# Last block's second layer in rounds of its own, its last stores on two queues; first block: a later load of the next x, weight joins in other slots

## The chip, the cores and the metric

The kernel runs on one core of one Trainium2 chip. The metric is the device time of one execution in microseconds (us), lower is better. The trace's span is about 1.8 us shorter than the device time of the same execution; where I follow one instruction I use the span's clock, which starts at zero with the first instruction. A transfer's landing is the moment when its counter says that it has finished; landings near the end of the kernel are taken to 0.01 us from the counters in the packed traces, since the views give them to 0.1. The close is the time from the last landing to the end of the span.

## The reference

A causal convolution over 7 steps, one softmaxed filter for each of 8 heads, then a two-layer network with hardswish:

```python
w = softmax(weight)                                    # (8, 7)
x1[b, s, d] = sum_k w[head(d), k] * x_padded[b, s + k, d]   # x: (8, 4096, 192)
h = x1.reshape(32768, 192) @ w_in                      # (192, 2048), float64 on input
g = h * clip(h + 3, 0, 6) / 6
out = g @ w_out                                        # (2048, 192), float64 on input
```

## The kernel before

The 32768 tokens go in 32 blocks of 1024. For each block VectorE convolves, TensorE makes h in PSUM banks (8 of 512 columns), ScalarE makes `r6 = relu(h/6 + 1/2)`, VectorE gates it (`g = min(r6, 1) * h`) and so frees the bank, and TensorE multiplies g by `w_out`. From block 1 on, both layers use Strassen's seven products instead of eight; block 0 is direct, since it also converts the weights. Words of 64 bits are loaded into `stage`, split on VectorE, scaled on ScalarE ("clamp"), joined on VectorE and multiplied on GpSimd, for 16 units: 0 to 7 are `w_in`, 8 to 15 `w_out`.

Block 0, the part that the change touches:

```python
swap(thirds[1]); split(3); split(4); join(2); clamp(3)   # join(n) also issues load(n + 4)
x_tiles[1] = load_x(1)
...
slots = [0, 1, 2, 3, 4, 6, 8, 10, 12, 14]    # a unit is joined in these slots
n = 3
for slot, (c, group) in enumerate(parts):    # slots 0 to 3 hold all 8 banks from the start
    ...                                      # TensorE: 6 matmuls into two banks
    def between():
        if more:
            join(n); clamp(n + 1)
    h_out(c, group, bs, ...)                 # two relus, between(), two gates that free the banks
    if more:
        split(n + 2)
        ...                                  # slots 0 to 3: between() comes here
        n += 1
```

The second layer of a later block, from which the last one differed only by having no next convolution:

```python
b, bank = three(1, 2, 0)       # one bank: product 1 on 96 partitions, a third of product 2 on 32
...
b, bank = three(4, 2, 1)
...                            # product 2's last third, in quarters of the contraction
b7, bank7 = three(7, 5, 0)
b, bank = three(6, 5, 1)
...                            # u2 = p1 + p6, u3 = u2 + p7, p4 = u3 - p4, store
b, bank = three(3, 5, 2)
piece(p5, 2, bank, NQ)         # ScalarE copies product 5's last third out of the bank
add(u2[:], u2[:], bank[m])     # VectorE, the other 96 partitions of the same bank
give(b)
add(u2[:], u2[:], p5[:])
store(u2, 0, 1)                # a transpose on VectorE, then three stores of 64 KB on SyncE's queue
add(u3[:], u3[:], p5[:])
store(u3, 1, 1)
```

Of the kernel before, what the change touches and what calls it, by code (L numbers as in the profile page):

```python
# [8 lines left out]
ALU = mybir.AluOpType  # L9
# [7 lines left out]
def kernel(  # L17
# [255 lines left out]
    def swap(part):  # L273

        to = slice(OTHER + part.start, OTHER + part.stop)
        nc.sync.dma_start(out=y[D2:P, to], in_=y[0:D2, part])
        nc.sync.dma_start(out=y[0:D2, to], in_=y[D2:P, part])
# [19 lines left out]
    def take():  # L297
        return free_banks.pop(0)
# [131 lines left out]
    def side_by_side(*streams):  # L430
        for mms in zip(*streams):
            for m in mms:
                m()

    every = range(NP)

    def store_rows(i, k, q, xt, j):

        t0 = i * TB + k * N
        nc.sync.dma_start(  # L440
            out=out[t0 : t0 + N, q * QS : (q + 1) * QS].rearrange("(t r) d -> r t d", r=QS),
            in_=xt[j * QS : (j + 1) * QS].rearrange("r (t d) -> r t d", d=QS),
        )
# [28 lines left out]
    def g_sums(engine, which, slots, width):  # L472
# [5 lines left out]
        for n in which:  # L478
            o, a, b, op = forms[n]
            for p in slots[::width]:  # L480
                r = slice(p, p + width)
                engine.tensor_tensor(out=o[:, r], in0=a[:, r], in1=b[:, r], op=op)  # L482

    def out_strassen(i, conv):

        prod = {
            1: (A11, B11), 2: (A12, B21), 3: (S4, B22), 4: (A22, T4),
            5: (S1, T1), 6: (S2, T2), 7: (S3, T3),
        }

        def product(bank, j, n, q, ks=every):
            return mm(bank, j, *prod[n], q, ks, True, True)

        def three(n, n4, q4):
            b = take()
            bank = psum[:, b]
            side_by_side(
                *[product(bank, q, n, q) for q in range(NQ)], product(bank, NQ, n4, q4)
            )
            return b, bank  # L500

        def piece(dst, q, src, j):
            nc.scalar.copy(  # L503
                out=dst[q * QS : (q + 1) * QS], in_=src[j * QS : (j + 1) * QS]
            )

        def add(out, x, y, op=ALU.add):
            nc.vector.tensor_tensor(out=out, in0=x, in1=y, op=op)  # L508

        def store(c, k, half_):  # L510

            xt = ot.tile([P, N], F32, name="xt")
            nc.vector.transpose(out=xt[0:DH], in_=c[:])  # L513
            for q in range(NQ):
                store_rows(i, k, half_ * NQ + q, xt, q)

        m = slice(0, DH)
        p1, p2, p4, p5, u2, u3 = (cs.tile([DH, N], F32, name=f"c{k}") for k in range(6))
        for u in conv:
            u()  # L520
        b, bank = three(1, 2, 0)
        nc.scalar.copy(out=p1[:], in_=bank[m])  # L522
        piece(p2, 0, bank, NQ)
        give(b)
        g_sums(nc.vector, (2,), every, 4)
        b, bank = three(4, 2, 1)
        nc.scalar.copy(out=p4[:], in_=bank[m])  # L527
        piece(p2, 1, bank, NQ)
        give(b)
        if conv:  # L530
            swap(slice(0, K3))
        n = NP // 4
        b = take()
        bank = psum[:, b]
        side_by_side(*[product(bank, j, 2, 2, range(j * n, (j + 1) * n)) for j in range(4)])
        last = slice(2 * QS, 3 * QS)
        piece(p2, 2, bank, 0)
        for j in range(1, 4):
            add(p2[last], p2[last], bank[j * QS : (j + 1) * QS])
        give(b)  # L540
        g_sums(nc.vector, (4,), every, 4)
        add(p2[:], p1[:], p2[:])
        store(p2, 0, 0)
        b7, bank7 = three(7, 5, 0)
        piece(p5, 0, bank7, NQ)
        if conv:
            y_sums()
        b, bank = three(6, 5, 1)
        piece(p5, 1, bank, NQ)
        add(u2[:], p1[:], bank[m])  # L550
        give(b)
        add(u3[:], u2[:], bank7[m])
        give(b7)
        add(p4[:], u3[:], p4[:], ALU.subtract)
        store(p4, 1, 0)
        b, bank = three(3, 5, 2)
        piece(p5, 2, bank, NQ)
        add(u2[:], u2[:], bank[m])
        give(b)
        add(u2[:], u2[:], p5[:])  # L560
        store(u2, 0, 1)
        add(u3[:], u3[:], p5[:])
        store(u3, 1, 1)

    def split(n):
        if n < len(units):
# [15 lines left out]
    with tc.manual_schedule():  # L582
        nc.vector.tensor_reduce(out=sm[:], in_=e_sb[:], axis=AX.X, op=ALU.add)
        nc.vector.tensor_scalar_add(sm[:], sm[:], 1e-9)
        nc.vector.reciprocal(sm[:], sm[:])
        nc.vector.tensor_tensor(
            out=c_sb[:], in0=e_sb[:], in1=sm[:].to_broadcast([P, KC]), op=ALU.mult
        )

        thirds = [slice(s, s + 1) for s in range(K3)]  # L590
        pe_third = K3 - 1
        b = take()
        for _ in range(3):

            nc.tensor.matmul(
                out=psum[:, b], lhsT=zeros[:, 0:P], rhs=zeros[:], start=True, stop=True
            )
        for k in range(KC):
            nc.scalar.mul(diag[:, k], ident[:], c_sb[:, k : k + 1])
            nc.tensor.matmul(  # L600
                out=psum[:, b], lhsT=diag[:, k], rhs=x_tiles[0][:, pe_third, k : k + N],
                start=(k == 0), stop=(k == KC - 1),
            )
        conv0 = conv_units(0, thirds[:pe_third], 2)
        per = len(conv0) // pe_third
        for k, u in enumerate(conv0):
            if k == 5:
                split(0)
                clamp(0)
            elif k == per - 3:  # L610
                join(0, more=False)
            elif k == per:
                nc.scalar.copy(out=y[:, pe_third], in_=psum[:, b])
                give(b)
                swap(thirds[0])
                swap(thirds[pe_third])
                load(AHEAD)
                split(1)
                clamp(1)
            elif k == per + 6:  # L620
                split(2)
                join(1)
                clamp(2)
            u()
        swap(thirds[1])
        split(3)
        split(4)
        join(2)
        clamp(3)
        x_tiles[1] = load_x(1)  # L630


        parts = [(c, group) for p in range(0, NP, 2) for group in (OWN, OTHER)
                 for c in (p, p + 1)]
        early = [(c, group, (take(), take())) for c, group in parts[:4]]
        order = (0, pe_third, 1)
        for c in range(2):
            for slot, group, bs in early:
                if slot == c:
                    for s in order[:2]:  # L640
                        h_mm(c, group, bs, s, order)
        for c, group, bs in early:
            h_mm(c, group, bs, order[2], order)

        slots = [0, 1, 2, 3, 4, 6, 8, 10, 12, 14]
        n = 3
        for slot, (c, group) in enumerate(parts):
            first = slot < len(early)
            if first:
                bs = early[slot][2]  # L650
            else:
                bs = take(), take()
                for s in range(K3):
                    h_mm(c, group, bs, s)
            more = slot in slots

            def between():
                if more:
                    join(n)
                    clamp(n + 1)  # L660

            h_out(c, group, bs, (lambda: None) if first else between)
            if more:
                split(n + 2)
                if first:
                    between()
                n += 1
        while n < len(units):
            join(n)
            clamp(n + 1)  # L670
            split(n + 2)
            n += 1
        w_sums()
        start_pools.close()
        ss = ctx.enter_context(tc.tile_pool(name="ss", bufs=1))
        p5s = ctx.enter_context(tc.tile_pool(name="p5s", bufs=3))
        cs = ctx.enter_context(tc.tile_pool(name="cs", bufs=1))
        ot = ctx.enter_context(tc.tile_pool(name="ot", bufs=4))

        def conv_and_swap(i):  # L680
            return conv_units(i, [slice(0, K3)]) + [lambda: swap(slice(0, K3)), y_sums]

        out_direct(0, conv_and_swap(1))
        x_tiles[2] = load_x(2)

        S1 = ss.tile([P, NP, N], F32, name="s1")[:]
        for i in range(1, NB):
            h_phase()
            out_strassen(i, conv_units(i + 1, [slice(0, K3)]) if i + 1 < NB else [])
            if i + 2 < NB:  # L690
                x_tiles[i + 2] = load_x(i + 2)

# [32 lines left out]
```

## Time and profile before

| | |
|---|---|
| time, median of 3 | 2446.81 us |
| TensorE busy | 2431.6 of 2444.9 us |
| TensorE idle before its first matmul / in block 0 / after its last | 1.5 / 3.5 / 8.3 us |
| second layer of block 0 begins | 60.94 us |
| last matmul ends | 2436.65 us |

The table is read as a budget: TensorE does the same work before and after, so only its idle time can change, and it lies at the two ends. The prediction below shows the lines.

### The profile page before, as it was taken

What the parts mean: (1) busy time and instruction counts of PE and PEld (TensorE: products, weight loads), DVE (VectorE), ACT (ScalarE), POOL (GpSimd) and SP (SyncE); (2) the same over time, 40 slices, a digit from 0 to 9 for tenths busy, and PEclk for the clock granted to TensorE, in tenths of its full rate; (3) what the DMA queues carried; (4) which work ended last, traced back from release to release, by engine and by line L of the source; (5) the groups of instructions that cost most, each with busy time, mean ns of one, the idle gap of its engine ahead of it and who ended that gap; (6) DMA issues with size and microseconds to landing.
All of it is one profiled execution on the core that took longest, in us unless ns stands there. A gap on an engine that the chain in (4) does not pass through costs nothing.

```text
span 2444.9 us, 40253 instructions
## 1 busy us (share of the span) xinstructions
PE 2431.6 (99%) x16468; PEld 1282.4 (52%) x16468; DVE 2089.3 (85%) x2532; ACT 1082.1 (44%) x1826; POOL 670.3 (27%) x280
## 2 busy tenths in 40 slices
PE   9999999999999999999999999999999999999998
PEld 4335554455554455544555445555455554455543
DVE  8788888988888888888888898888888888888885
ACT  7234553345443355433454334543335543345432
POOL 2423321233221333122332123322133312233222
PEclk9999999999999999999999999999999999999999
DMA  5211121101122111111112211122201122111210
GB/s 143 40 26 28 27 40 40 39 18 27 36 40 40 21 33 27 40 40 23 30 27 40 40 34 23 24 40 40 40 19 35 27 40 40 21 33 27 40 27 14
DMA packets 227338, 84.67 MB, mean 35 GB/s; under 512 B 205456, under 2 KB 210576, under 8 KB 227152
## 3 DMA queue, kind: packets, MB, share of 16 engines
q1 hardware_dynamic: 226904, 81.69, 16.7%
q8 instruction: 129, 2.11, 0.4%
q14 instruction: 57, 0.47, 0.1%
q0 software_dynamic: 96, 0.26, 0.0%
q10 hardware_dynamic: 152, 0.13, 0.0%
HBM read 31.72 MB, written 25.17 MB: 23 GB/s over the span
## 4 chain that ended last, share of the span: by engine, by line
PE 98%; DVE 1%; DMA 0%; issue 0%; SPq 0%; ACTq 0%; POOL 0%; ACT 0%; DVEq 0%
PE psum L311 51%; PE psum L422 48%; DMA stage<-in_moe_w_in_dram 0%; DVE y L263 0%; DMA x<-in_x_dram 0%; DVE sig L199 0%; DVE c L508 0%; DVE scale L195 0%; DVE scale L174 0%; DVE g L321 0%; DVE top L178 0%; ACTq L92 0%; POOL w_in L203 0%; DVE y L259 0%; DVE xt L513 0%
## 5 line engine op out<-in xcount | busy, mean ns | idle before, releaser
L422 PE MATMUL psum<-g,w_out 128*32 128x512 f32 x9312 | 1165.2, 592 | 0.0
L311 PE MATMUL psum<-y,w_in 64*128 64x512 f32 x3664 | 980.9, 591 | 3.5 <-DVE g L321 1.3
L422 PEld LDWEIGHTS psum<-g,w_out 128*32 128x32 f32 x9312 | 337.8, 110 | 812.9 <-issue 764.8
L482 POOL TENSOR_TENSOR s<-g 128x1024 f32<-128x1024 f32 x124 | 293.4, 2366 | 1676.3 <-DVE g L321 1632.2
L317 ACT ACTIVATE r<-psum,half 128x512 f32<-128x512 f32 x1024 | 637.1, 687 | 245.9 <-PE psum L311 242.9
L311 PEld LDWEIGHTS psum<-y,w_in 64*128 64x128 f32 x3664 | 615.3, 187 | 194.7 <-issue 69.2
L321 DVE SCALAR_TENSOR_TENSOR g<-r,psum 128x512 f32<-128x512 f32 x1024 | 642.6, 680 | 4.6 <-ACT r L317 1.8
L422 PE MATMUL psum<-s,w_out 128*32 128x512 f32 x1488 | 643.6, 592 | 0.0
L311 PE MATMUL psum<-y,w_in_t 64*128 64x512 f32 x1984 | 639.2, 595 | 0.0
L391 DVE TENSOR_TENSOR psum<-psum,p 128x512 f32<-128x512 f32 x496 | 320.9, 692 | 209.1 <-PE psum L311 202.1
L263 DVE SCALAR_TENSOR_TENSOR y<-x,c_sb,y 128x1536 f32<-128x1536 f32 (+1 forms) x210 | 416.7, 1991 | 6.6
L311 PEld LDWEIGHTS psum<-y,w_in_t 64*128 64x128 f32 x1984 | 336.1, 187 | 138.1 <-issue 28.2
L503 ACT COPY c<-psum 32x512 f32<-32x512 f32 x186 | 107.6, 578 | 602.4 <-PE psum L422 601.7
L482 POOL TENSOR_TENSOR g<-g 128x1024 f32<-128x1024 f32 x124 | 336.4, 2713 | 9.7
L508 DVE TENSOR_TENSOR c<-c,psum 32x512 f32<-32x512 f32 (+1 forms) x186 | 127.4, 685 | 103.1 <-ACT c L503 98.0
L384 ACT COPY psum<-psum 128x512 f32<-128x512 f32 x248 | 138.6, 571 | 64.9 <-PE psum L311 52.6
L387 ACT COPY p<-psum 128x512 f32<-128x512 f32 x248 | 141.8, 586 | 54.9 <-PE psum L311 51.4
L422 PEld LDWEIGHTS psum<-s,w_out 128*32 128x32 f32 x1488 | 163.7, 110 | 0.0
L482 DVE TENSOR_TENSOR g<-s,g 128x2048 f32<-128x2048 f32 x62 | 141.1, 2316 | 2.2 <-PE psum L422 2.2
L482 DVE TENSOR_TENSOR g<-g 128x2048 f32<-128x2048 f32 x62 | 139.3, 2288 | 1.0
L522 ACT COPY c<-psum 96x512 f32<-96x512 f32 x31 | 18.0, 581 | 197.4 <-PE psum L422 197.4
L527 ACT COPY c<-psum 96x512 f32<-96x512 f32 x31 | 18.0, 581 | 175.7 <-PE psum L422 175.7
(45 smaller groups left out, 433.4 us busy)
## 6 DMA issues: line engine op xcount, KB each, us to landing
out_dram<-xt SPq DMA_DIRECT2D x384, 64.0 KB, 2.0
y<-y SPq DMA_DIRECT2D x62, 384.0 KB, 4.9
x<-in_x_dram SPq DMA_DIRECT2D x55, 388.5 KB, 5.5
stage<-in_moe_w_in_dram SPq DMA_DIRECT2D x16, 192.0 KB, 5.3
stage<-in_moe_w_out_dram SPq DMA_DIRECT2D x8, 384.0 KB, 6.3
x<-in_x_dram SPq DMA_DIRECT2D x7, 384.0 KB, 4.7
y<-y SPq DMA_DIRECT2D x6, 128.0 KB, 2.3
x<-in_x_dram SPq DMA_DIRECT2D x2, 128.0 KB, 4.4
```

The costliest lines, as they stand in the source:

```text
L263: nc.vector.scalar_tensor_tensor(out=to, in0=x[:, part, k + t : k + t + W], scalar=c, in1=to, op0=ALU.mult, op1=ALU.add,)
L311: nc.tensor.matmul(out=psum[:, b], lhsT=w[r], rhs=y[r, third_of_y], start=start, stop=stop, skip_group_check=onto,)
L317: nc.scalar.activation(r6, h, ACT.Relu, bias=half[:], scale=1.0 / 6.0)
L321: nc.vector.scalar_tensor_tensor(out=out, in0=r6, scalar=1.0, in1=h, op0=ALU.min, op1=ALU.mult)
L384: nc.scalar.copy(out=psum[:, bank["b"]], in_=psum[:, bank["a"]])
L387: nc.scalar.copy(out=self.p5[:], in_=psum[:, bank["e"]])
L391: nc.vector.tensor_tensor(out=psum[:, to], in0=psum[:, bank["b"]], in1=self.p5[:], op=ALU.add)
L422: lambda p=p: nc.tensor.matmul(out=bank[j * QS : (j + 1) * QS], lhsT=w_out[:, p, w, cols], rhs=x[:, p], start=(first and p == ps_[0]), sto ...
L482: engine.tensor_tensor(out=o[:, r], in0=a[:, r], in1=b[:, r], op=op)
L503: nc.scalar.copy(out=dst[q * QS : (q + 1) * QS], in_=src[j * QS : (j + 1) * QS])
L508: nc.vector.tensor_tensor(out=out, in0=x, in1=y, op=op)
L522: nc.scalar.copy(out=p1[:], in_=bank[m])
```

## The change

The intent is to shorten both ends. In block 0 the next block's x is loaded behind the weights, which are more urgent, and the fourth join is moved one slot back. In the last block, which has no next convolution to serve, the products go in another order, so that only one add and a transpose stand between the last matmul and most of the stores, and these go out on two queues. The core of the diff; the helper functions moved out of `out_strassen`, with little change (`store` now takes its rows and queues):

```diff
-    def store_rows(i, k, q, xt, j):
+    def store_rows(i, k, q, xt, j, dma=nc.sync):
...
+    def out_last(i):
+        both = nc.sync, nc.scalar
...                                   # rounds (1 with a third of 2) and (two thirds of 2, of 4)
+        b7, bank7 = three(7, 5, 0)
+        piece(p5, 0, bank7, NQ)
+        b, bank = three(6, 5, 1)
+        piece(p5, 1, bank, NQ)
...                                   # u2, u3, two thirds of p4, two stores
+        b, bank = by_quarters(5, 2)
+        pieces(p5, 2, bank)
+        give(b)
+        add(u2[:], u2[:], p5[:])
+        add(p5[:], u3[:], p5[:])
+        store(i, p5, 1, 1)
+        b, bank = three(3, 4, 2)
+        add(u2[:], u2[:], bank[m])
+        store(i, u2, 0, 1, queues=both)
+        add(u3[rows(2)], u3[rows(2)], bank[rows(NQ)], ALU.subtract)
+        store(i, u3, 1, 0, range(2, 3), queues=both[::-1])
+        give(b)
...
-        x_tiles[1] = load_x(1)
...
-        slots = [0, 1, 2, 3, 4, 6, 8, 10, 12, 14]
+        slots = [0, 1, 2, 3, 5, 6, 8, 10, 12, 14]
...
+            if slot == 6:
+                x_tiles[1] = load_x(1)
             h_out(c, group, bs, (lambda: None) if first else between)
```

More of the change, by code (lines that the diff above doesn't have):

```diff
@@ L435 @@
     every = range(NP)
-    def store_rows(i, k, q, xt, j):
+    def store_rows(i, k, q, xt, j, dma=nc.sync):
         t0 = i * TB + k * N
-        nc.sync.dma_start(
+        dma.dma_start(
             out=out[t0 : t0 + N, q * QS : (q + 1) * QS].rearrange("(t r) d -> r t d", r=QS),
@@ L482, in g_sums @@
                 engine.tensor_tensor(out=o[:, r], in0=a[:, r], in1=b[:, r], op=op)
-    def out_strassen(i, conv):
-        prod = {
-            1: (A11, B11), 2: (A12, B21), 3: (S4, B22), 4: (A22, T4),
-            5: (S1, T1), 6: (S2, T2), 7: (S3, T3),
-        }
-        def product(bank, j, n, q, ks=every):
-            return mm(bank, j, *prod[n], q, ks, True, True)
-        def three(n, n4, q4):
-            b = take()
-            bank = psum[:, b]
-            side_by_side(
-                *[product(bank, q, n, q) for q in range(NQ)], product(bank, NQ, n4, q4)
-            )
-            return b, bank
-        def piece(dst, q, src, j):
-            nc.scalar.copy(
-                out=dst[q * QS : (q + 1) * QS], in_=src[j * QS : (j + 1) * QS]
-            )
-        def add(out, x, y, op=ALU.add):
-            nc.vector.tensor_tensor(out=out, in0=x, in1=y, op=op)
-        def store(c, k, half_):
-            xt = ot.tile([P, N], F32, name="xt")
-            nc.vector.transpose(out=xt[0:DH], in_=c[:])
-            for q in range(NQ):
-                store_rows(i, k, half_ * NQ + q, xt, q)
-        m = slice(0, DH)
-        p1, p2, p4, p5, u2, u3 = (cs.tile([DH, N], F32, name=f"c{k}") for k in range(6))
@@ new lines, with product, four, three @@
+    prod = {
+        1: (A11, B11), 2: (A12, B21), 3: (S4, B22), 4: (A22, T4),
+        5: (None, T1), 6: (S2, T2), 7: (S3, T3),
+    }
+    def product(bank, j, n, q, ks=every):
+        x, w = prod[n]
+        return mm(bank, j, S1 if n == 5 else x, w, q, ks, True, True)
+    def four(*parts):
+        b = take()
+        bank = psum[:, b]
+        side_by_side(*[product(bank, j, n, q) for j, (n, q) in enumerate(parts)])
+        return b, bank
+    def three(n, n4, q4):
+        return four(*[(n, q) for q in range(NQ)], (n4, q4))
@@ new lines, in by_quarters, with rows, piece, pieces @@
+    def by_quarters(n, q):
+        b = take()
+        bank = psum[:, b]
+        w = NP // 4
+        side_by_side(
+            *[product(bank, j, n, q, range(j * w, (j + 1) * w)) for j in range(4)]
+        )
+        return b, bank
+    def rows(q):
+        return slice(q * QS, (q + 1) * QS)
+    def piece(dst, q, src, j):
+        nc.scalar.copy(out=dst[rows(q)], in_=src[rows(j)])
+    def pieces(dst, q, src):
+        piece(dst, q, src, 0)
+        for j in range(1, 4):
+            add(dst[rows(q)], dst[rows(q)], src[rows(j)])
@@ new lines, in add, with store, sums_tiles @@
+    def add(out, x, y, op=ALU.add):
+        nc.vector.tensor_tensor(out=out, in0=x, in1=y, op=op)
+    def store(i, c, k, half_, qs=range(NQ), queues=(nc.sync,)):
+        xt = ot.tile([P, N], F32, name="xt")
+        r = slice(qs[0] * QS, (qs[-1] + 1) * QS)
+        nc.vector.transpose(out=xt[r], in_=c[r])
+        for q in qs:
+            store_rows(i, k, half_ * NQ + q, xt, q, queues[q % len(queues)])
+    def sums_tiles():
+        return (cs.tile([DH, N], F32, name=f"c{k}") for k in range(6))
@@ new lines @@
+    m = slice(0, DH)
+    def out_last(i):
+        both = nc.sync, nc.scalar
+        p1, p2, p4, p5, u2, u3 = sums_tiles()
+        b, bank = three(1, 2, 0)
+        nc.scalar.copy(out=p1[:], in_=bank[m])
+        piece(p2, 0, bank, NQ)
+        give(b)
+        g_sums(nc.vector, (2,), every, 4)
+        b, bank = four((2, 1), (2, 2), (4, 0), (4, 1))
+        for dst, q, j in ((p2, 1, 0), (p2, 2, 1), (p4, 0, 2), (p4, 1, 3)):
+            piece(dst, q, bank, j)
+        give(b)
+        g_sums(nc.vector, (4,), every, 4)
+        add(p2[:], p1[:], p2[:])
+        store(i, p2, 0, 0)
+        b7, bank7 = three(7, 5, 0)
+        piece(p5, 0, bank7, NQ)
+        b, bank = three(6, 5, 1)
+        piece(p5, 1, bank, NQ)
+        add(u2[:], p1[:], bank[m])
+        give(b)
+        add(u3[:], u2[:], bank7[m])
+        give(b7)
+        two = slice(0, 2 * QS)
+        add(p4[two], u3[two], p4[two], ALU.subtract)
+        store(i, p4, 1, 0, range(2))
+        b, bank = by_quarters(5, 2)
+        pieces(p5, 2, bank)
+        give(b)
+        add(u2[:], u2[:], p5[:])
[6 more added lines that the diff above has]
+        store(i, u3, 1, 0, range(2, 3), queues=both[::-1])
+        give(b)
@@ L519, in out_strassen @@
+    def out_strassen(i, conv):
+        p1, p2, p4, p5, u2, u3 = sums_tiles()
         for u in conv:
@@ L529, in out_strassen @@
         give(b)
-        if conv:
-            swap(slice(0, K3))
-        n = NP // 4
-        b = take()
-        bank = psum[:, b]
-        side_by_side(*[product(bank, j, 2, 2, range(j * n, (j + 1) * n)) for j in range(4)])
-        last = slice(2 * QS, 3 * QS)
-        piece(p2, 2, bank, 0)
-        for j in range(1, 4):
-            add(p2[last], p2[last], bank[j * QS : (j + 1) * QS])
+        swap(slice(0, K3))
+        b, bank = by_quarters(2, 2)
+        pieces(p2, 2, bank)
         give(b)
@@ L542, in out_strassen @@
         add(p2[:], p1[:], p2[:])
-        store(p2, 0, 0)
+        store(i, p2, 0, 0)
         b7, bank7 = three(7, 5, 0)
         piece(p5, 0, bank7, NQ)
-        if conv:
-            y_sums()
+        y_sums()
         b, bank = three(6, 5, 1)
@@ L554, in out_strassen @@
         add(p4[:], u3[:], p4[:], ALU.subtract)
-        store(p4, 1, 0)
+        store(i, p4, 1, 0)
         b, bank = three(3, 5, 2)
@@ L560, in out_strassen @@
         add(u2[:], u2[:], p5[:])
-        store(u2, 0, 1)
+        store(i, u2, 0, 1)
         add(u3[:], u3[:], p5[:])
-        store(u3, 1, 1)
+        store(i, u3, 1, 1)
     def split(n):
@@ L688 @@
             h_phase()
-            out_strassen(i, conv_units(i + 1, [slice(0, K3)]) if i + 1 < NB else [])
+            if i + 1 < NB:
+                out_strassen(i, conv_units(i + 1, [slice(0, K3)]))
+            else:
+                out_last(i)
             if i + 2 < NB:
```

## The prediction

> **What bounds the kernel now.** I read the page's head first, then TensorE's order of time over the first 100 us, then VectorE, ScalarE and the SyncE queue in the same stretch, then the chain that ended last over the final 10 us.
>
> ```profile
> span 2444.9 us, 40253 instructions
> PE 2431.6 (99%) x16468; PEld 1282.4 (52%) x16468; DVE 2089.3 (85%) x2532; ACT 1082.1 (44%) x1826; POOL 670.3 (27%) x280
> ```
>
> TensorE is idle for 2444.9 - 2431.6 = 13.3 us in all. The table of stretches gives TensorE 2300.00 of 2300.00 us between 100 and 2400 us at a granted clock of 1.00, so whatever the 30 middle blocks do, a change that leaves their matmuls alone gains nothing there. The 13.3 us lie at the ends: 1.5 before the first matmul, some 3.5 in the first block, 8.3 after the last matmul. These are the whole purse, 0.5% of the time. A gain over 2% (49 us) is out of reach unless matmuls vanish; they don't (counted below).
>
> The first block, TensorE (start, duration; idle before, and its releaser, in brackets):
>
> ```profile
> 25.19 9.74 PE L311 MATMUL psum<-y,w_in 64*128 64x512 f32 x44 [0.18 <-DMA y<-y]
> 35.94 3.44 PE L311 MATMUL psum<-y,w_in 64*128 64x512 f32 x12 [1.01 <-DVE g L321]
> 39.64 21.37 PE L311 MATMUL psum<-y,w_in 64*128 64x512 f32 x96 [0.26 <-DVE g L321]
> ```
>
> One slot of the loop (one chunk, one group) is 12 of these records; the weight loads come in pairs every 0.43 us, so a slot takes 6 x 0.43 = 2.57 us. Slot 4 begins at about 27.0 (25.19 plus eight records of slots 2 and 3), so slot 8 should begin at 27.0 + 4 x 2.57 = 37.3. It begins at 39.64: 2.3 us are lost, more than the two brackets say (1.27), since a slot that waits for its second bank also runs stretched (3.44 us for 12 records). All 8 banks are taken by slots 0 to 3, so slots 7 and 8 wait for the gates (L321) of slots 3 and 4. VectorE shows why these are late:
>
> ```profile
> 33.71 0.36 DVE L174 TENSOR_SCALAR scale<-stage 128x384 uint32<-128x384 uint32 x1 [1.68 <-DMA stage<-in_moe_w_in_dram]
> 35.20 1.29 DVE L321 SCALAR_TENSOR_TENSOR g<-r,psum 128x512 f32<-128x512 f32 x2
> 37.87 0.56 DVE L195 SCALAR_TENSOR_TENSOR scale<-stage,scale 128x384 uint32<-128x384 uint32 x1
> 38.33 0.56 DVE L199 SCALAR_TENSOR_TENSOR sig<-top,sig 128x384 f32<-128x384 uint32 x1
> 38.80 1.28 DVE L321 SCALAR_TENSOR_TENSOR g<-r,psum 128x512 f32<-128x512 f32 x2
> ```
>
> It waits 1.68 us for the last w_in words (unit 7), and then does the join of unit 7 (37.87 and 38.33) ahead of slot 4's gates. The words are late because of the queue:
>
> ```profile
> 24.89 0.53 SPq L85 DMA_DIRECT2D x<-in_x_dram  x1
> 25.47 0.60 SPq L86 DMA_DIRECT2D x<-in_x_dram  x1
> 26.12 1.25 SPq L137 DMA_DIRECT2D stage<-in_moe_w_in_dram  x2
> ```
>
> The two x transfers (388.5 KB each) are ahead of unit 7 in issue, and the 16 DMA engines are full between 26 and 31 us (212 to 250 GB/s). ScalarE, meanwhile, has no room to spare:
>
> ```profile
> 34.11 0.62 ACT L186 ACTIVATE sig<-scale,bias_e 128x384 f32<-128x384 uint32 x1
> 35.86 1.25 ACT L317 ACTIVATE r<-psum,half 128x512 f32<-128x512 f32 x2
> ```
>
> It runs back to back from 24 to 52 us: two relus (1.14 us from start to next start) and a clamp (1.75) in each slot with a join, 2.89 against TensorE's 2.57.
>
> The end of the kernel, the chain that ended last, and the last line of the SyncE queue:
>
> ```profile
> 2436.67 0.59 ACT c L503
> 2437.28 0.69 DVE c L508
> 2438.00 0.70 DVE c L508
> 2438.72 0.04 DVE xt L513
> 2439.36 0.66 DVE c L508
> 2440.04 0.71 DVE xt L513
> 2441.99 0.51 SPq L440 DMA_DIRECT2D out_dram<-xt  x1
> ```
>
> The last matmul ends at 2436.65. Then come a ScalarE copy, two adds and a transpose, another add and transpose, and six stores on one queue, issued from 2439.46 to 2441.99 some 0.5 apart. From the start of the last issue to the end of the span are 2.91 us (landing 2.0, then the close).
>
> **What the Trainium skill says.** "PSUM — Partial Sum Buffer", section "PSUM bank collisions raise a hardware error": two engines on one bank and 32-partition quadrant at once raise an error, reads against reads too, and software keeps them apart. The trace agrees as to order: the add on the last bank, which needs nothing of ScalarE's copy, starts at 2437.28, 0.03 after that copy ends, though the two read different partitions of the bank. "DMA: Bandwidth & Descriptors", section "Issuing engines are not separate DMA queues": stores from two engines share the same 16 DMA engines, and a second issuer saves only sequencer time. In the trace that time is the 0.5 us an issue above. "Perfetto Trace Analysis", section "Identifying the Most-Contended Engine": matmul busy share is no measure of roofline. I use it only to locate gaps, and take the pace from weight loads.
>
> **The change, part by part.** The last block: matmul counts. Before, five rounds of 32 and a quarter round of 8; after, four rounds of 32 around products (1,2), (2,4), (7,5), (6,5), then 8 for product 5, then 32: 168 matmuls either way, the same 36.2 us. What changes is what is left after the last. Product 5 is now complete before it, and the last bank is read by VectorE alone.
>
> From the last matmul at 2436.65 (old clock): no copy, so the add starts at 2436.67 in place of 2437.28 (gain 0.61). The second add (0.72 from start to start) is done earlier. Transpose from 2437.39 to 2438.10, the first stores at 2438.13 on two queues. VectorE goes on at 2438.03 with a 32x512 add (0.65, as L508) and a transpose (0.71; adds and copies cost the same at 32 and 96 partitions, 0.69 and 0.58, so I take the 96-partition time): ends at 2439.4. Old end of that last transpose: 2440.75. Its single store goes out on ScalarE's queue at once, at 2439.45, in place of the third of a row at 2441.99. Plus 2.91: 2442.35 against 2444.9. The gain is 2.5 us: 0.61 copy, 0.72 add, 1.2 queue (2441.99 - 2440.75).
>
> Is VectorE free at 2436.67? Round (6,5) ends at 2428.1; copy to 2428.7, adds u2, u3, p4 and a transpose at 0.7 each to 2431.5, three adds of quarters to 2433.6, two more to 2435.0, a transpose to 2435.7. One microsecond spare. Its three stores keep SyncE until about 2437.2, before 2438.1.
>
> The first block. With x moved to slot 6, unit 7 is issued at 24.9 in place of 26.1 and has 777 KB less ahead of it; at 230 GB/s it lands near 30, before VectorE asks at 32.0. The wait of 1.68 goes. But only part of it was binding: slot 3's gates also need ScalarE's relu, which started at 32.94, so they can start at 33.65, not 33.5; TensorE's slot 7, due at 34.74, then loses only about 0.2 on the second bank. Slot 4's gates need relu 4, which still starts at 35.83, as the clamp ahead of it starts at 34.08 in place of 34.11. So the gates run from 36.53 to 37.8 (the join of unit 7, 0.93, no longer in front), and slot 8 begins near 37.8, not 39.64. Its own ideal was 37.3; ScalarE keeps 0.5. From there: gates 5 end at 39.95 (wanted 40.4), gates 6 at 42.6 (43.0), gates 7 at 44.75 (45.5), then ever more room. Gain 1.85 us.
>
> All after it is TensorE without a gap, so it arrives whole at the end if nothing fixed in time stands in the way. The last w_out unit is multiplied by 68.9, moves up with the gates, and is wanted at about 71. The next convolution needs x at about 66; x now lands near 40. The sums of weights end at 90.3, before block 1 at 100.
>
> Sum: 1.85 + 2.5 = 4.35. 2446.81 - 4.35 = 2442.5.
>
> **Rivals.** (1) ScalarE takes the wait's place in full: slots 7 and 8 stay late because ScalarE is saturated. For it: the back-to-back run and relu 4 at 35.86. Against: relu 3 started at 32.94, while its gates waited until 35.20. If it holds, the first block gains 0.5 or less and the time is 2443.8. (2) The first block's gain is given back at the next join of streams: if the spread joins or the later x hold up w_out or the convolution, TensorE waits around 70 or 100. The margins are 2 us or more, so I give this 10%; time 2444.3. (3) The stores don't gain: the transfers bunch up. Six of 64 KB move at about 120 GB/s, 0.5 each, so four need some 2.1 us from 2438.9, to 2441.0, before the last landing I expect at 2441.5. It could cost 0.3. (4) The opposite: the slots recover all 2.3 us and the landings quicken with fewer stores: 2441.8.
>
> **Range and chances.** The tail is nearly arithmetic (2.2 to 2.8); the first block can be 0.5 to 2.3. Together 2.7 to 5.1 with the likely mass at 3.5 to 4.8; I take 2441.6 to 2443.9. All that is within 0.25%; 2% would need 49 us, nowhere in sight.
>
> **What would show it.** Right: no wait for the stage transfer at VectorE near 32; TensorE at slot 8 near 37.8 and the second layer beginning near 59.1 in place of 60.94; last matmul at about 2434.8; span end some 5.7 us after it in place of 8.25; about 2440.5 in all. Wrong: a new TensorE gap between 38 and 105 us, or around product 5's quarter round; a VectorE still busy with that quarter when the last round ends; a slower issue or landing on ScalarE's queue.

## The result, and the profile after

The changed kernel takes 2442.53 us (median of 6, 2442.31 to 2442.66), the kernel before 2446.71 in the same rounds (2446.45 to 2446.94): 4.18 us less, a ratio of 0.9983 (95% interval 0.997 to 0.9996). A ratio is the mean time of one kernel's runs over that of the other's of the same rounds, so it isn't quite the ratio of the medians. The predicted time was 2442.5.

The head of the page after:

```profile
span 2440.7 us, 40261 instructions
PE 2430.1 (100%) x16468; PEld 1282.7 (53%) x16468; DVE 2091.1 (86%) x2534; ACT 1083.5 (44%) x1827; POOL 671.4 (28%) x280
```

The count of matmuls in the trace is the same. Idle time of TensorE falls from 13.3 to 2440.7 - 2430.1 = 10.6 us; some of the gain is in the spacing of matmuls that count as busy, so the starts are the better measure. TensorE's order of time after, in block 0 (start, duration, group; idle before and its releaser in brackets):

```profile
17.16 41.68 PE L311 MATMUL psum<-y,w_in 64*128 64x512 f32 x184 [0.82 <-DMA y<-y]
58.77 41.41 PE L422 MATMUL psum<-g,w_out 128*32 128x512 f32 x384
```

Where two groups waited for VectorE's gates (at 35.94 and 39.64), one group now runs through from 17.16 to the second layer, which begins at 58.77 in place of 60.94: 2.17 us earlier. VectorE, same columns:

```profile
32.00 0.35 DVE L174 TENSOR_SCALAR scale<-stage 128x384 uint32<-128x384 uint32 x1
...
33.74 1.29 DVE L321 SCALAR_TENSOR_TENSOR g<-r,psum 128x512 f32<-128x512 f32 x2 [0.17 <-ACT r L317]
...
36.64 1.28 DVE L321 SCALAR_TENSOR_TENSOR g<-r,psum 128x512 f32<-128x512 f32 x2
37.84 0.55 DVE L195 SCALAR_TENSOR_TENSOR scale<-stage,scale 128x384 uint32<-128x384 uint32 x1
```

The wait for the stage transfer is gone (L174 starts at 32.00 without one, in place of 33.71), slot 3's gates now wait for ScalarE (0.17), slot 4's gates run at 36.64 in place of 38.80, and the join of unit 7 (L195) comes behind them. The SyncE queue:

```profile
23.48 2.55 SPq L137 DMA_DIRECT2D stage<-in_moe_w_in_dram  x4
26.08 2.13 SPq L145 DMA_DIRECT2D stage<-in_moe_w_out_dram  x4
28.39 0.55 SPq L85 DMA_DIRECT2D x<-in_x_dram  x1
```

Four halves of w_in units go out without a break; the later of unit 7's, issued at 25.43, lands after 4.0 us, at 29.4.

The chain that ended last, over the end, and then the line of ScalarE's queue for the last store:

```profile
2434.51 0.69 DVE c L526
2435.23 0.04 DVE xt L532
2435.97 0.70 DVE c L526
2436.69 0.70 DVE xt L532
```

```profile
2437.43 0.32 ACTq L440 DMA_DIRECT2D out_dram<-xt  x1
```

The last matmul ends at 2434.49, 2.16 us earlier than before: block 0's gain arrived whole. ScalarE's copy and one add are gone from the chain. From the last matmul to the end of the span it takes 2440.7 - 2434.49 = 6.21 us in place of 8.25, a gain of 2.04, not the 2.5 predicted. What is odd is the close. The last store lands 1.8 after its issue, at 2439.21, and the span ends 1.48 later. Before, the last store landed 2.0 after its issue at 2441.99, at 2443.98, and the span ended 0.95 later.

### The profile page after: what moved, and what is told of

Same layout as the page of the kernel before. It is cut to its first block, busy times and chain, and to the rows that moved or that the text cites. A ratio compares the mean times of both kernels' runs of the same rounds, so it can differ in the third digit from the quotient of the medians.

```text
span 2440.7 us, 40261 instructions
## 1 busy us (share of the span) xinstructions
PE 2430.1 (100%) x16468; PEld 1282.7 (53%) x16468; DVE 2091.1 (86%) x2534; ACT 1083.5 (44%) x1827; POOL 671.4 (28%) x280
## 4 chain that ended last, share of the span: by engine, by line
PE 99%; DVE 1%; DMA 0%; issue 0%; ACTq 0%; SPq 0%; DVEq 0%
PE psum L311 51%; PE psum L422 48%; DVE y L263 0%; DMA x<-in_x_dram 0%; DMA y<-y 0%; DVE c L526 0%; ACTq L92 0%; DVE scale L174 0%; DVE y L259 0%; DVE sig L199 0%; DVE scale L195 0%; DVE top L178 0%; DVE xt L532 0%; SPq L276 0%; DVEq L259 0%
```

## The experiments

There were twelve runs of eleven kernels, each of five executions, one of them profiled; all gave the right result. "Before" in the same rounds had medians of 2446.47 to 2446.75 and spread over 0.5 to 1.05 us, so gains are read from the medians of the kernels and from the traces together.

**first_only.** The changed kernel with the old last block on one queue.

```diff
     def out_last(i):
-        ...                       # the new rounds
+        ...                       # the old rounds, all stores on SyncE's queue
```

> Only the first block's part of the change (x behind more results, joins spread); the last block in the old order on one queue. If the two ends add up: TensorE reaches the second layer of block 0 at 58.77 as in the changed kernel, all after shifts by 2.17 us, the tail after the last matmul is 8.25 us as before, the time is about 2444.55. Rival (the first block's gain is partly given back in the middle, and what the traces show of it belongs to the last block): last matmul later than 2434.8, time above 2445.3.

Measured: 2444.52 us (before: 2446.47). The second layer of block 0 begins at 58.84, the last matmul ends at 2434.54, the tail is 8.26. The first block's gain is its own and reaches the end whole.

**tail_only.** The changed kernel with x's load and the join slots as before.

```diff
+        x_tiles[1] = load_x(1)             # ahead of the slots, as before
-        slots = [0, 1, 2, 3, 5, 6, 8, 10, 12, 14]
+        slots = [0, 1, 2, 3, 4, 6, 8, 10, 12, 14]
-            if slot == 6:
-                x_tiles[1] = load_x(1)
```

> Only the last block's part; first block as before. If the two ends add up: second layer of block 0 at 60.94, last matmul at 2436.65, tail 6.2 us, time about 2444.7 (gain 2.05). Rival: as the prediction has it, the tail alone gives 2.5 us and the time is 2444.2; then the shorter figure in the changed kernel's trace was an accident of one execution.

Measured: 2444.54 us (before: 2446.47). Last matmul at 2436.41, end at 2442.6: 6.19, as in the changed kernel (6.21). The close is 1.48. So the missing 0.5 us was no accident of one execution. The two singles gain 1.95 and 1.93, 3.9 together; both together gained 4.18 in other rounds, within what the kernel before scatters.

**load_only.** Only the later load of x.

```diff
-        slots = [0, 1, 2, 3, 5, 6, 8, 10, 12, 14]      # first_only otherwise
+        slots = [0, 1, 2, 3, 4, 6, 8, 10, 12, 14]
```

> Of the first block's part only the later load of x; joins in the old slots; old last block. Theory (the join of unit 7 ahead of slot 4's gates costs by itself once the wait for the stage transfer is gone): VectorE's wait of 1.68 us is gone, slot 4's gates begin near 37.4 in place of 36.6, slot 8 of TensorE near 38.1, gain about 1.5 us, time about 2445.2. Rival (ScalarE is so full that the wait did not bind): gain 0.5 or less, time 2446.2 or more. Second rival (the later load is all there is): gain 2.17, time 2444.55.

Measured: 2445.16 in the profiled execution, 2445.82 to 2445.98 in the four others. The profiled one is what the theory says: no wait for the transfer, slot 4's gates at 37.30, slot 8 at 38.13, the second layer at 59.43. The others are 0.7 us slower.

**load_only_again.** The same kernel, unchanged.

> The kernel with only the later load of x, once more, unchanged: its profiled execution ran 2445.16, as its theory has it, but the four others 2445.82 to 2445.98. If the kernel has two ways to run that an accident of transfer timing picks, the executions fall near 2445.2 and 2445.9 again, in another mix. If the profiled execution was a single outlier, all five are near 2445.9, the profile shows VectorE waiting or slot 8 at about 38.9 in place of 38.1, and the load alone is worth 0.6 to 0.8.

Measured: 2446.09 to 2446.22 four times, the profiled one among them, and 2445.26 once. So there are two ways to run. Apart from a shift of some 0.1 us, the two traces differ first in the join of unit 7. VectorE in the faster trace, with the gates after it and an instruction of the next split:

```profile
36.83 0.56 DVE L199 SCALAR_TENSOR_TENSOR sig<-top,sig 128x384 f32<-128x384 uint32 x1
37.30 1.29 DVE L321 SCALAR_TENSOR_TENSOR g<-r,psum 128x512 f32<-128x512 f32 x2
38.49 0.94 DVE L174 TENSOR_SCALAR scale<-stage 128x384 uint32<-128x384 uint32 x1
```

GpSimd in the same trace, the multiply of unit 6:

```profile
36.53 1.72 POOL L203 TENSOR_TENSOR w_in<-sig,scale 128x384 f32<-128x384 f32 x1 [1.91 <-DVE sig L199]
```

In the slower one, VectorE and then GpSimd:

```profile
36.94 1.36 DVE L199 SCALAR_TENSOR_TENSOR sig<-top,sig 128x384 f32<-128x384 uint32 x1
38.23 1.27 DVE L321 SCALAR_TENSOR_TENSOR g<-r,psum 128x512 f32<-128x512 f32 x2
```

```profile
36.64 1.25 POOL L203 TENSOR_TENSOR w_in<-sig,scale 128x384 f32<-128x384 f32 x1 [1.90 <-DVE sig L199]
```

With two joins back to back, VectorE joins unit 7 while GpSimd multiplies unit 6, and one of the two is held up. In the faster trace it is GpSimd (1.72 in place of 1.00), and VectorE pays only after the gates (0.94 in place of 0.35, while GpSimd multiplies unit 7). In the slower one it is VectorE, by 0.8 (1.36 in place of 0.56), just ahead of the gates that TensorE waits for: its slot 8 begins at 39.05 in place of 38.13. The Trainium skill has this in "SBUF — State Buffer", section "Who interferes with whom": a VectorE instruction with two inputs in SBUF and a GpSimd instruction that reads SBUF use the same port, and the one issued first makes the other wait. L199 has two such inputs; in the slower trace it starts at 36.94, when GpSimd is at work, and ends 0.41 after GpSimd does, which agrees. In the faster trace GpSimd also starts before L199 (36.53 and 36.83), and yet it is GpSimd that is held up; so these starts don't tell who will wait, and what tips it is not shown. It is shown that the collision separates these two traces; that the other eight executions split for the same reason is inferred from their times. The trace of the kernel before has the collision too, in the form of the faster trace (GpSimd's multiply at 38.04 takes 1.71, the split at 40.00 takes 0.93).

**slots_only.** Only the join slots, x loaded early as before.

```diff
+        x_tiles[1] = load_x(1)             # ahead of the slots, as before; first_only otherwise
-            if slot == 6:
-                x_tiles[1] = load_x(1)
```

> Of the first block's part only the join slots (5 in place of 4); x is loaded early as before; old last block. Theory: the wait of 1.68 us stays, slot 7 begins at 35.94 as before, slot 4's gates begin at 37.9 in place of 38.8, slot 8 near 38.6, gain about 1.0 us, time about 2445.7. With the load alone at 1.5 the two singles would sum to 2.5, more than the 2.17 together, since ScalarE's relu of slot 4 at 35.9 is the floor under both. Rival (the slots matter only once the words come in time): gain under 0.2, time 2446.5.

Measured: 2445.66 us (before: 2446.47), a gain of 0.8; in the trace slot 4's gates at 37.83, the second layer at 59.97, 0.97 earlier. The theory holds. The slot change works by itself even with the words late, and it does a second thing that nobody had priced: with the joins of units 6 and 7 two microseconds apart, the collision of the last experiment doesn't arise in its trace. One of its five executions was still 0.4 us faster than the others (2445.21), for a reason that was not looked for.

**one_queue.** The changed kernel with all its stores on SyncE's queue.

```diff
-        store(i, u2, 0, 1, queues=both)
+        store(i, u2, 0, 1)
-        store(i, u3, 1, 0, range(2, 3), queues=both[::-1])
+        store(i, u3, 1, 0, range(2, 3))
```

> The changed kernel with its last four stores all on SyncE's queue. The last store's issue is at 2.94 us after the last matmul either way (VectorE's last transpose ends then, and SyncE is done with the three others 0.05 before). Theory A (the close is longer when the last store went out on ScalarE's queue, or when two queues are open: 3.27 us from the last issue to the end against 2.91 before): the close falls back to about 2.9, the kernel is some 0.3 us faster than the changed one, 2442.2. Theory B (the landings are slower because four transfers bunch): no change, 2442.5. Theory C (the second queue pays as intended): slower by 0.1 to 0.5, since the third of the row is issued later.

Measured: 2442.04 us, 0.5 less than the changed kernel. The last store is issued at 2437.63 (2.98 after the last matmul at 2434.65; with two queues it was 2.94), lands 1.9 later, and the span ends 0.91 after that. The second queue did not pay; without it the close is back at 0.9.

**last_on_sync.** Only the very last store moved to SyncE's queue.

```diff
-        store(i, u3, 1, 0, range(2, 3), queues=both[::-1])
+        store(i, u3, 1, 0, range(2, 3))
```

> The changed kernel with only the very last store moved to SyncE's queue; the middle of the three before it stays on ScalarE's. Theory A in the form 'the last store's queue matters': as with one queue, about 2442.2. In the form 'a second queue in use at the end costs': as the changed kernel, 2442.5. Theory B: 2442.5.

Measured: 2441.85 us (2441.82 to 2441.99; before: 2446.75; ratio 0.9981). It beats both kernels: 0.7 us less than the changed one, and 0.2 less than one_queue, so one store on the second queue may be worth a little. The last store on SyncE's queue in its trace:

```profile
2437.44 0.32 SPq L440 DMA_DIRECT2D out_dram<-xt  x1
```

It is issued 0.01 after its fellow in the changed kernel (2437.43, above), lands after the same 1.8, and yet the span ends at 2440.1 in place of 2440.7. So neither issue nor landing makes the difference; the close does (0.91 against 1.48). Theory A looked right here; a later run limits it.

**old_order_two_queues.** The first block's part, the old rounds, the last six stores alternating over both queues.

```diff
-        store(i, u2, 0, 1)                             # first_only otherwise
+        store(i, u2, 0, 1, queues=(nc.sync, nc.scalar))
-        store(i, u3, 1, 1)
+        store(i, u3, 1, 1, queues=(nc.scalar, nc.sync))
```

> The changed kernel's first block, and the last block's rounds in the old order, but its last six stores alternating over two queues. The chain up to the last transpose stays (4.1 us after the last matmul), only the 1.2 us of queue behind it go, if the queue is worth what the prediction says: last issue near 4.5 after the last matmul in place of 5.34, end at some 7.6 in place of 8.25; against the kernel with only the first block's part (2444.55) faster by 0.4 to 0.9: about 2443.9. Rival (queue time is hidden by the landings, which share the DMA engines): same as that kernel within 0.1.

Measured: 2444.31 us, against 2444.52 for the same kernel on one queue; the tail is 2442.4 - 2434.35 = 8.05 against 8.26. The last issue does start earlier, 4.54 after the last matmul in place of 5.34, but the landings stretch from 2.0 to 2.5 us. Of 0.8 us of issue, 0.2 arrive. This is nearer the rival: what the second issuer saves is spent in landing.

**copy_back.** One ScalarE copy put back on the last bank.

```diff
         b, bank = three(3, 4, 2)
+        piece(p4, 2, bank, NQ)
         add(u2[:], u2[:], bank[m])
...
-        add(u3[rows(2)], u3[rows(2)], bank[rows(NQ)], ALU.subtract)
+        add(u3[rows(2)], u3[rows(2)], p4[rows(2)], ALU.subtract)
```

> The changed kernel with one ScalarE copy put back on the last bank: product 4's last third is copied out first, and VectorE's last add reads the copy in place of the bank. The adds on the other 96 partitions need nothing of it. If the wait of the old tail (0.61) was one for the bank and not for data, VectorE's first add starts 0.6 later again, and the kernel is slower than the changed one by 0.5 to 0.6: about 2443.1. Rival (the two read different partitions and run side by side): no change, 2442.5.

Measured: 2443.09 us, 0.56 more than the changed kernel. VectorE's first add in the tail, in its trace:

```profile
2435.05 0.68 DVE L526 TENSOR_TENSOR c<-c,psum 96x512 f32<-96x512 f32 x1 [1.38 <-ACT c L518]
```

The last matmul ended at 2434.42, so the add starts 0.63 after it (0.02 in the changed kernel) and is released by the copy, whose result it doesn't use. The old tail's wait was one for the bank.

**one_add.** The last bank added in one instruction over 128 partitions.

```diff
+        add(all4[m], u2[:], p5[:])                     # earlier, in place of u2 += p5
+        nc.scalar.copy(out=all4[rows(NQ)], in_=u3[rows(2)])
...
-        add(u2[:], u2[:], bank[m])                     # and the second add, both stores
+        nc.vector.scalar_tensor_tensor(                # sign: +1 on 96 partitions, -1 on 32
+            out=all4[:], in0=bank, scalar=sign[:], in1=all4[:], op0=ALU.mult, op1=ALU.add)
+        nc.vector.transpose(out=xt[:], in_=all4[:])
+        ...                                            # four stores: SyncE, ScalarE, SyncE, ScalarE
```

> The changed kernel with its last bank added in one instruction over all 128 partitions (a sign per partition), one transpose of 128 partitions, and the four last stores two on each queue. It takes 1.44 us of VectorE (the second add and transpose) off the chain after the last matmul. If VectorE and the issue bound the end, the last issue ends 0.9 after the transpose on ScalarE's queue in place of 1.8, and with 2.95 from there to the end it gains 0.9: about 2441.6. Rival (the transfers bound it: four of 64 KB at some 0.5 each, now all at once, as in the old tail's six): the landings stretch from 1.8 to 2.5 or more and the gain is 0.5 or less: about 2442.0 to 2442.5.

Measured: 2442.83 us, 0.3 more than the changed kernel and above both forecasts. The single transpose ends at 2436.08, 1.3 earlier than the changed kernel's second, but the four stores now go out together. The list of transfers has ScalarE's later store with its size in KB and its time from issue to landing in us, first in the changed kernel:

```profile
out_dram<-xt ACTq DMA_DIRECT2D x1, 64.0 KB, 1.8
```

and in this one:

```profile
out_dram<-xt ACTq DMA_DIRECT2D x1, 64.0 KB, 2.8
```

It is issued at 2436.54 and lands at 2439.35, no earlier than the changed kernel's 2439.21. The transfers took the place of VectorE. The close is 1.48 again.

**one_add_31.** The same, three of the four stores on SyncE's queue.

```diff
-            store_rows(i, k, q, xt, j, (nc.sync, nc.scalar)[j % 2])
+            store_rows(i, k, q, xt, j, nc.scalar if j == 1 else nc.sync)
```

> The same single add and transpose, three of the last four stores on SyncE's queue and one, the second, on ScalarE's, so that no late issue is on ScalarE's. If the close is 2.34 after SyncE's last issue (in four kernels so far) and 2.95 after ScalarE's: end 3.75 after the transpose, against 4.16 in the kernel whose very last store alone went to SyncE: about 2441.45. If the transfers bound it: end 4.2 after the transpose, 2441.85, the same as that kernel.

Measured: 2442.22 us. From the transpose's end at 2436.17 to the end of the span it takes 4.27 us, as the transfer-bound theory says (4.2). But that theory expected the time of last_on_sync, 2441.85, and this is 0.4 slower in time and 0.23 in the tail of the trace (5.87 after the last matmul against 5.64): here the transpose ends 1.60 after the last matmul, there the first one ends 1.45 after it, and the rest of the 0.4 is not explained.

**halves_spread.** The last round in two halves of 256 columns, stores of 32 KB.

```diff
+        store(i, p5, 1, 1, queues=(nc.sync, nc.scalar))
+        ...
+        for h in range(2):
+            cols = slice(h * half_n, (h + 1) * half_n)
+            b, bank = four_cols(cols, (3, 0), (3, 1), (3, 2), (4, 2))
+            ...                            # signed add, transpose, four stores of these columns
```

> An attempt to beat both kernels: the last round's matmuls in two halves of 256 columns, each on its own bank, each followed by one signed add and one transpose over 128 partitions, and stores of 32 KB, spread over both queues with the very last three on SyncE's. Half of the bytes then leave while TensorE still works. If the end is bound by the bytes that leave after the last matmul (256 KB in the changed kernel, 128 KB here) and by VectorE (two instructions of some 0.4 in place of four of 0.7): last transpose near 0.9 after the last matmul, last landing near 4.3 after it, close 0.9: end 5.0 to 5.3 after the last matmul in place of 6.2 (5.6 with the last store on SyncE's queue), time 2441.3 to 2441.6. Rival (issue: eight stores cost as many issues at half the size; the stores before them hold the queues): 2441.8 or more. Second rival (TensorE: with 256 columns the weight loads no longer hide): last matmul later by 0.5 or more, time 2442.3.

Measured: 2442.15 us. TensorE doesn't suffer (the two halves take 7.09 us, the same round in the changed kernel 7.05), and the last transpose ends 1.07 after the last matmul in place of 2.90. But SyncE's queue is full of small stores, and the last one is issued only at 2437.12, 2.75 after the last matmul. It lands 1.6 later, at 2438.76, and the close is 1.51. The time is that of the rival (issue), but its cause is only half right: the landing comes 4.39 after the last matmul, close to the 4.3 of the first theory and 0.33 earlier than in the changed kernel, and it is the close, 1.51 where 0.9 was expected, that takes the gain.

This run also breaks the simple form of theory A: its last store is on SyncE's queue, and the close is long all the same. The packed traces hold SyncE's closing instructions, which no view prints. SyncE waits for eight counters of finished transfers, one after another, in an order that ends with 4, 5, 6, 7, then come two instructions named DRAIN and a few of GpSimd's. From the start of the second DRAIN to the end of the span it takes 0.76 or 0.77 us in every trace but one (copy_back, 0.89), so nearly all of the difference lies before it. Where the last landing is the one that counter 7 counts, the close is 0.91 to 0.98 (before, all runs in the old order on one queue, one_queue, last_on_sync, one_add_31). Where it is on 5 (changed, tail_only, one_add), 6 (copy_back) or 3 (halves_spread), it is 1.40 to 1.51. Only old_order_two_queues, on 6, has 0.97.

The traces show where the extra time goes. In the five with the long close SyncE still goes through the counters behind the last landing, at some 0.07 each, and after that landing it pauses once for 0.34 between two closing instructions (0.05 is usual), with nothing outstanding that the trace shows; in four of the five a DRAIN also takes 0.13 in place of 0.01. In last_on_sync and one_queue the same pause stands ahead of the last landing (2438.66 to 2438.99 and 2438.36 to 2438.70), where it costs nothing; in old_order_two_queues none follows the last landing. So the close is long where the pause falls behind the last landing. What the pause is, and what sets its place, stays open; that the last store's queue sets it, through the place of its counter in SyncE's order, was not shown.

## Why the prediction was right

Total right: 2442.5 predicted, 2442.53 measured. But two errors of opposite sign cancelled in part (first block 0.32 too low, tail 0.46 too high), and the kernel before ran 0.1 us faster in these rounds than in the earlier ones; that the total agrees to 0.03 us is luck. The parts are worth more than the sum. (By its own parts, 2.7 to 5.1, the stated range would have been 2441.7 to 2444.1, not 2441.6 to 2443.9.)

*The purse.* TensorE's idle ends were the whole of what could be gained, and the middle did not move: right. The last matmul shifted by 2.16 us, exactly what the second layer of block 0 shifted.

*First block, predicted 1.85, measured 2.17.* The mechanism was right to the tenth: the wait for unit 7's words gone, relu 3 then the floor under slot 3's gates (0.17 of wait in the trace), relu 4 still at 35.9, the gates of slot 4 at 36.64 where 36.53 was predicted. What was mis-sized is the step "slot 8 begins near 37.8, not 39.64". The old 39.64 is the start on the first bank of two; the 37.8 was the moment of the second bank. Like for like, the weight loads of slot 8 start at 37.44 in place of 39.61, and that difference is the 2.17. Rival 1 (ScalarE takes the wait's place) is excluded by first_only. Rival 2 (given back later) did not occur. That load and slots both matter is shown by the singles: in the traces the load alone gains 1.5 where it ran the faster way (second layer at 59.43) and 0.6 where it ran the slower (60.34), the slots alone 0.97, both 2.1.

*The tail, predicted 2.5, measured 2.04.* This is outside the 2.2 to 2.8 that the prediction gave for the tail and called nearly arithmetic. The copy's 0.61 was right, and copy_back shows it (0.61 in the trace, 0.56 in time). The second add is gone from the chain and the order of rounds held, VectorE was free 0.77 before the last bank was ready where about 1.0 was reckoned, and the last issue starts 2.94 after the last matmul where 2.80 was predicted: the 32x512 add starts 0.74 after the transpose before it, not 0.64. The step that failed is "Plus 2.91", from the last issue to the end. It was carried over as a constant and measured 3.26 (before, read to 0.01 us, 2.94), made up of a shorter landing (1.8 in place of 2.0) and a longer close (1.48 in place of 0.95). And "1.2 queue" was credited to the two queues; one_queue shows that the new order alone takes it (its tail is 5.75 us, against 8.26 in the old order): with fewer stores after the last bank, SyncE's queue is free in time, and the same kernel with one queue is 0.5 us faster. Rival 3 (transfers bunch) was set at 0.3; with six stores on two queues it ate 0.6 of 0.8 us. Rival 4 came half true: the slots recovered 2.17 of their 2.3 and the landing was 0.2 shorter, but the longer close took more than that back.

One reading of the skill goes too far. The two reads of the last bank (ScalarE's copy on 32 partitions, VectorE's add on the other 96) fall in different quadrants, so the rule that the prediction cites doesn't require their order. The trace shows that this build keeps them apart all the same.

## What to carry to other kernels

When an engine is busy for 99% of the span, the gain is in its idle ends, and there a tenth of a microsecond is settled by comparing the same event before and after (first bank with first bank), not by the moment that happens to be in the table. A second queue for the last stores is worth only the issue time that no landing hides, and reordering so that fewer bytes leave after the last result can make it needless: try it with and without, and look at how long the program runs on after the last landing. Two producers that share a port, run back to back, can make a kernel run in two ways; spread them.

## What the Trainium skill lacked or had wrong

- No page says that the program's own end varies with the last stores: from the last landing to the end of the span 0.91 to 0.98 us in nine traces here, 1.40 to 1.51 in five others; moving one store between queues was worth 0.7 us. "Runtime: NRT & Kernel Launch" would be the place.
- "DMA: Bandwidth & Descriptors", section "Issuing engines are not separate DMA queues", is right that a second issuer saves only sequencer time, but has no figure for how much of it is lost again: with six stores of 64 KB the last issue came 0.8 us earlier and the end 0.2.
- "PSUM — Partial Sum Buffer", section "PSUM bank collisions raise a hardware error", says that two engines may access different 32-partition quadrants of one bank at once; this kernel's build orders ScalarE's and VectorE's reads of one bank even so, and that cost 0.61 us at the end. The page could warn of the cost.
